# Two changes to a fused recurrence and gated MLP: four products alternate over TensorE's quadrants, and three of six inversions use 16-wide substitution

## The chip, the cores and the metric

The kernel runs on one core of one Trainium2 chip. Its time is the device time of one execution in microseconds (us); the figure for a version is the median of its runs. The engines are called as in the profile: PE is TensorE (its weight loads are PEld), DVE is VectorE, ACT is ScalarE, POOL is GpSimd and SP is the engine that issues DMAs.

## The reference

Inputs `r, k, v, w, a, b` have the shape 4 x 8 x 768 x 40 (batch, heads, tokens, head width), fp32. Each of the 32 (batch, head) pairs has a 40 x 40 state that is carried over 768 tokens. The output of that recurrence, 4 x 768 x 320, goes through a gated MLP with a product over the tokens:

```python
for t in range(S):
    y[:, :, t] = einsum('bhd,bhde->bhe', rt, state)
    Sa = einsum('bhde,bhe->bhd', state, at)
    state_decay = state * wt[:, :, None, :] - einsum('bhd,bhe->bhde', Sa, bt)
    state = state_decay + einsum('bhd,bhe->bhde', vt, kt)
x = y.transpose(0, 2, 1, 3).reshape(4, 768, 320)
h = maximum(x @ w_in, 0)                       # 320 -> 1024
u, v = h[..., :512], h[..., 512:]
v_n = (v - mean(v)) / sqrt(var(v) + 1e-6)
v_s = einsum('ts,bsd->btd', w_spatial, v_n) + b_spatial[None, :, None]
out = ((u * v_s) @ w_out)                      # 512 -> 320
```

## The kernel before

**Tiling.** The tokens of a sequence are cut into 12 chunks of 64 (`C`). Two batches run together, so that there are 24 steps (`NS`), each with one chunk of 16 (batch, head) pairs: 8 units (`NU`) on partitions 0 to 63 and 8 on 64 to 127. A half of the partitions is called `par`, and its rows `PR[par]`. In a product the two halves use either the two quadrants of TensorE on the diagonal (rows and columns of the same half) or the two others (rows of one half, output in the other).

**Inside a chunk** the recurrence becomes a triangular system. Its 64 x 64 unit lower triangle is split in two blocks of 32 (`HB`). The strict lower parts of the diagonal blocks of 4 chunks (`GS`), 32 units for each of four 32-row strips, stand in one tile `Lc` (`lprime`, L318, and `lblock`, L332). `invert(g)` (L342) inverts them for a group of 4 steps on DVE: it transposes `Lc` so that one unit's matrix lies along the free dimension of a partition, does forward substitution in place with 30 pairs of a product and a sum (L351, L355), and transposes the result twice, into `XT0` (L360) and `X11` (L362). Group 0 is inverted ahead of the steps. Groups 1 to 5 are generators whose pieces are spread over the steps before their use. `b_l21`, `b_zt`, `b_xcopy` and `b_x21` (L452 to L513) build the full 64 x 64 inverse `xf` from the two blocks; `b_x21` needs `zt`, which ACT copies out of PSUM in `b_zt_out` (L486).

**A step `s`** is a chain: `c_bp` (products with the state `Mc`, L535, diagonal quadrants), `c_ff` (L553), `c_xx` (with the inverse, L571, diagonal quadrants), `c_mp` (state update, L603) with `c_mp_out` on DVE, and `c_y` (L627) with `c_y_out` on DVE (L640), which frees the PSUM tile that the next step's `c_bp` writes. ACT copies each product out of PSUM (`c_bp_out` L545, `c_ff_out` L561, `c_xx_out` L582), and POOL's `strict` (L396) zeroes the upper triangle of some of them. For the step that follows, the same step forms `b_lka` (L389, operands `sl` and `at`; the two quadrants off the diagonal) and `b_h` (L419, operand `lin`; also off the diagonal). Each has its drain, `b_lka_out` (L406) and `b_h_out` (L429): two ACT copies and two `strict` on POOL.

**Preparation.** `scan1`, `scan2`, `at_mul` and `sl_mul` (L281 to L313) prepare chunks 4 to 23 on DVE, two per step up to step 3 and then one. `decode` turns the 64-bit `w_in` into a pair of fp32r values on DVE in steps 4 to 10. From step 11 the MLP's first product fills PE (`m_u` L742, `m_v` L697), one piece at each of the four times `M1` to `M4` of a step. What is left of it, and phase 2 (`spatial` L173 to L180 and `proj` L193), follows the last step.

**What sets the order.** In phase 1 the order of every engine's queue is written out: `at(t, fn, ...)` enters a call at time `t` in units of steps, the list is sorted, and the calls are issued in that order. [...] The times of this kernel for a step `s`: `c_bp` 0.00 and 0.05 for its two groups of 4 units, `b_lka` 0.115, `b_lka_out` 0.17 and 0.19, `c_ff` 0.30 and 0.35, `c_xx` 0.55 and 0.60, `c_xx_out` 0.60 and 0.65, `b_zt` 0.66, `b_h` 0.68, `b_zt_out` 0.68, `b_h_out` 0.72 and 0.74, `c_mp` 0.74 and 0.76, `b_x21` 0.78, `c_y` 0.86 and 0.90. In steps 3, 7, 11, 15 and 19, where the next step begins a group, `b_zt` is at 0.88 and `b_x21` at 1.12. Behind the last step the order is the scheduler's. PSUM tiles of `ps_k` (two buffers) are shared by `lprime`, `b_lka`, `b_h`, `b_tok`, `b_l21`, `b_zt` and `b_x21`.

Of the kernel before, what the change touches and what calls it, by code (L numbers as in the profile page):

```python
# [211 lines left out]
def phase1(ctx, tc, early, late, vtok, win, xs, vns, uts, dscr):  # L212
# [39 lines left out]
    maskp = const.tile([P, C], F32, name="maskp")
    maskn = const.tile([P, C], F32, name="maskn")
# [87 lines left out]

    def invert(g):  # L342
        Lc = st.pop(("Lc", g))
# [3 lines left out]
        nc.vector.memset(A.rearrange("p t s -> p (t s)")[:, 0:HB * HB:HB + 1], 1.0)
        for k in range(1, HB - 1):
            m = HB - 1 - k
            tp = ps_i.tile([P, m, k], F32, name="itmp")  # L350
            nc.vector.tensor_tensor(  # L351
                out=tp, in0=A[:, k + 1:, k:k + 1].broadcast_to([P, m, k]),
                in1=A[:, k:k + 1, 0:k].broadcast_to([P, m, k]), op=ALU.mult,
            )
            nc.vector.tensor_tensor(out=A[:, k + 1:, 0:k], in0=A[:, k + 1:, 0:k], in1=tp, op=ALU.add)  # L355
# [4 lines left out]
        nc.vector.transpose(out=XT0.rearrange("p u t -> p t u"), in_=A)  # L360
        yield
        nc.vector.transpose(out=X11.rearrange("p u t -> p t u"), in_=A.rearrange("p t s -> p s t"))  # L362
# [20 lines left out]

    def b_lka(s):
        Et, at, sl = st["pre", s]
        pk = ps_k.tile([P, NU, C], F32, name="bk")
        for n in range(NU):
            for par in range(2):
                nc.tensor.matmul(  # L389
                    pk[PR[1 - par], n, :], lhsT=sl[PR[par], n, 1 - par, :], rhs=at[PR[par], n, :],  # L390
                    start=True, stop=True,
                )
        st["pk", s] = pk

# [6 lines left out]
    def b_lka_out(s, par):  # L401
        At = st["blk", s][0]
        pk = st["pk", s]
        ev = PR[1 - par]
        if s in LKA_POOL:
            nc.scalar.activation(At[par][ev], pk[ev], AF.Copy)  # L406
            strict(At[par][ev], NU)
            return
        nc.vector.tensor_tensor(
            out=At[par][ev], in0=pk[ev],  # L410
            in1=maskp[ev].unsqueeze(1).broadcast_to([64, NU, C]), op=ALU.mult,
        )

    def b_h(s):
# [1 line left out]
        ph = ps_k.tile([P, NU, C], F32, name="bk")
        for n in range(NU):
            for par in range(2):
                nc.tensor.matmul(  # L419
                    ph[PR[1 - par], n, :], lhsT=li[RR[par], n, 0:C], rhs=li[RR[par], n, C:2 * C],  # L420
                    start=True, stop=True,
                )
        st["ph", s] = ph

    def b_h_out(s, par):
        ev = PR[1 - par]
        Rt = Rts[s % 2]
        if s in H_POOL:
            nc.scalar.activation(Rt[par][ev, :, 0:C], st["ph", s][ev], AF.Copy)  # L429
            strict(Rt[par][ev, :, 0:C], NU)  # L430
            return
        nc.vector.tensor_tensor(
            out=Rt[par][ev, :, 0:C], in0=st["ph", s][ev],
            in1=maskp[ev].unsqueeze(1).broadcast_to([64, NU, C]), op=ALU.mult,
        )

# [92 lines left out]
    def c_bp(s, g):  # L529
        gp, ns = grp(g)  # L530
        li = lin[s % 2]
        bp = ps_b.tile([P, NP, NR], F32, name=f"bp{g}")
        for q, n in enumerate(ns):
            for par in range(2):
                nc.tensor.matmul(  # L535
                    bp[PR[par], q, :], lhsT=Mc[RR[par], n, :], rhs=li[RR[par], n, C:],
                    start=(q == 0), stop=False, skip_group_check=True,
                )
# [37 lines left out]
    def c_xx_out(s, g):  # L576
        gp, ns = grp(g)
        Rt = st["blk", s][1]
        xx = st["xx", g]
        if s in TRI_POOL:  # L580
            for par in range(2):
                nc.scalar.activation(Rt[par][PR[par], gp], xx[PR[1 - par]], AF.Copy, scale=-1.0)  # L582
            for par in range(2):
                strict(Rt[par][PR[par], gp, 0:C], NP)
            return
        for par in range(2):
            nc.scalar.activation(Rt[par][PR[par], gp, C:], xx[PR[1 - par], :, C:], AF.Copy, scale=-1.0)
        for par in range(2):
            ur, ev = PR[par], PR[1 - par]
            nc.vector.tensor_tensor(  # L590
                out=Rt[par][ur, gp, 0:C], in0=xx[ev, :, 0:C],
                in1=maskn[ev].unsqueeze(1).broadcast_to([64, NP, C]), op=ALU.mult,
            )

# [264 lines left out]
    with tc.manual_schedule():  # L859
# [20 lines left out]
        for m, val in ((maskp, 1.0), (maskn, -1.0)):  # L880
            p.memset(m, val)
            for rows in PR:
                p.affine_select(
                    out=m[rows], in_=m[rows], pattern=[[1, C]], base=0,
                    channel_multiplier=-1, compare_op=ALU.is_gt, fill=0.0,
                )
        for t in (Mc, *xfs):
# [110 lines left out]
```

## Time and profile before

| | |
|---|---|
| median of 3 runs | 706.14 us (703.38 to 710.57) |
| the profiled execution | 708.83 us, of it 707.1 us span |
| mean granted PE clock | 0.897 |
| PE, DVE, ACT, POOL busy | 584.4, 444.9, 387.8, 297.9 us |
| DMA | 87.66 MB, mean 124 GB/s |

Busy time is the union of an engine's instructions. The page shows the span in 40 equal slices (17.7 us each), a digit being a tenth of busy time. In a row of busy time by stretch there follow the stretch, its length, and for PE, PEld, DVE, ACT and POOL the busy us and in brackets the number of instructions; then the granted clock, the share of the DMA engines and GB/s. In a row of the timeline stand start, duration, engine, line, operation, output and inputs and the number of instructions; in square brackets the idle time before it and what ended it. "issue" means that no semaphore ended it. In a row of a group of instructions stand the busy time and the mean ns of one, and then the idle time before them.

### The profile page before, as it was taken

How to read it: one execution, taken by the hardware profiler on the slowest of the kernel's cores; microseconds unless marked ns; L12 is line 12 of the kernel's file. 1: busy time of each engine (PE TensorE's matmuls, PEld its weight loads, DVE VectorE, ACT ScalarE, POOL GpSimd, SP SyncE). 2: the span in 40 equal slices, each digit the busy share in tenths (PEclk: the TensorE clock that was granted, in tenths of full speed). 3: DMA queues.
4: the chain of work that ended last, by engine and by line, in shares of the span. 5: the costliest groups of instructions: out<-in, count | busy, mean ns of one | idle time of the engine just before them, and what ended most of it. 6: DMA issues, size and time to landing. Idle time of an engine off the chain costs nothing. (4 is left out here: it accounts for less than half of the span.)

```text
span 707.1 us, 25562 instructions
## 1 busy us (share of the span) xinstructions
PE 584.4 (83%) x10784; PEld 533.2 (75%) x10784; DVE 444.9 (63%) x884; ACT 387.8 (55%) x856; POOL 297.9 (42%) x486
## 2 busy tenths in 40 slices
PE   1716786477776786999998999989999999999997
PEld 1605675467666785888877788778888989999997
DVE  7898679987999999877777466611127521322221
ACT  2406463355555765587866888887855543331112
POOL 5202132113445455354653434544448982553221
PEclk9656898868887888799997999998999999999999
DMA  9562758366564644666547545454336464650001
GB/s 186 97 118 47 145 114 164 63 132 123 123 129 106 147 91 111 133 147 139 115 135 220 128 135 148 121 157 119 107 106 187 143 179 135 189 178 28 29 29 57
DMA packets 105179, 87.66 MB, mean 124 GB/s; under 512 B 34344, under 2 KB 90920, under 8 KB 103144
## 3 DMA queue, kind: packets, MB, share of 16 engines
q1 hardware_dynamic: 104520, 84.31, 48.7%
q10 hardware_dynamic: 544, 1.72, 1.1%
q8 instruction: 85, 1.39, 0.9%
q14 instruction: 30, 0.25, 0.1%
HBM read 59.20 MB, written 20.50 MB: 113 GB/s over the span
## 5 line engine op out<-in xcount | busy, mean ns | idle before, releaser
L396 POOL TENSOR_SCALAR_AFFINE_SELECT Rt<-Rt 64x512 f32<-64x512 f32 (+1 forms) x144 | 85.1, 592 | 105.6 <-ACT Rt L582 73.9
L545 ACT ACTIVATE Rt<-bp 64x416 f32<-64x416 f32 x96 | 49.2, 513 | 72.6 <-PE bp L535 71.0
L396 POOL TENSOR_SCALAR_AFFINE_SELECT At<-At 64x512 f32<-64x512 f32 x48 | 42.1, 877 | 83.1 <-ACT At L406 68.3
L351 DVE TENSOR_TENSOR itmp<-A 128x30 f32<-128x30 f32 (+9 forms) x180 | 70.6, 392 | 3.3
L535 PE MATMUL bp<-lin,Mc 40*64 40x104 f32 x768 | 53.6, 305 | 22.1 <-DVE y L640 21.5
L535 PEld LDWEIGHTS bp<-lin,Mc 40*64 40x64 f32 x768 | 47.0, 169 | 25.0 <-DVE y L640 24.0
L173 PE MATMUL pg<-wsh,vh 128*128 128x384 f32 x192 | 64.7, 337 | 0.0
L174 PE MATMUL pg<-wsl,vh 128*128 128x384 f32 x192 | 64.7, 337 | 0.0
L175 PE MATMUL pg<-wsh,vl 128*128 128x384 f32 x192 | 64.6, 336 | 0.0
L355 DVE TENSOR_TENSOR A<-A,itmp 128x30 f32<-128x30 f32 (+9 forms) x180 | 59.1, 328 | 6.2
L177 DVE TENSOR_TENSOR g<-pg,bb 128x384 f32<-128x384 f32 x32 | 17.8, 556 | 64.6 <-PE pg L175 59.2
L54 POOL TENSOR_TENSOR gl<-g,gh 128x384 fp32r<-128x384 f32 x32 | 33.9, 1063 | 49.9 <-ACT gh L50 49.7
L582 ACT ACTIVATE Rt<-ch 64x416 f32<-64x416 f32 x96 | 49.2, 513 | 3.9 <-PE ch L571 1.5
L553 PE MATMUL ch<-Rt,At 128*64 128x104 f32 x768 | 48.5, 287 | 0.0
L553 PEld LDWEIGHTS ch<-Rt,At 128*64 128x64 f32 x768 | 43.0, 160 | 4.4 <-issue 1.7
L326 PE MATMUL bk<-at,sl 64*32 64x32 f32 x1536 | 22.3, 210 | 27.4 <-DVE sl L313 14.7
L571 PE MATMUL ch<-ffs,xf 64*64 64x104 f32 x768 | 43.4, 266 | 1.1 <-issue 1.1
L477 PE MATMUL bk<-XT,l 32*32 32x32 f32 x768 | 18.3, 198 | 30.8 <-DVE XT L360 27.7
L54 POOL TENSOR_TENSOR vl<-raw,vh 128x512 fp32r<-128x512 f32 x24 | 32.1, 1344 | 27.2 <-ACT vh L50 22.2
L50 ACT ACTIVATE gh<-g 128x384 fp32r<-128x384 f32 x32 | 16.6, 523 | 48.7 <-DVE g L178 48.7
L477 PEld LDWEIGHTS bk<-XT,l 32*32 32x32 f32 x768 | 15.5, 113 | 35.1 <-issue 23.5
L326 PEld LDWEIGHTS bk<-at,sl 64*32 64x32 f32 x1536 | 18.8, 121 | 30.6 <-DVE sl L313 14.8
(134 smaller groups left out, 1580.9 us busy)
## 6 DMA issues: line engine op xcount, KB each, us to landing
ein<-in_early SPq DMA_DIRECT2D x40, 387.0 KB
lin<-in_late SPq DMA_DIRECT2D x48, 160.0 KB
At<-at SPq DMA_DIRECT2D x48, 128.0 KB
uts<-ur SPq DMA_DIRECT2D x48, 128.0 KB
vns<-vr SPq DMA_DIRECT2D x24, 256.0 KB
raw<-vns SPq DMA_DIRECT2D x24, 256.0 KB
ut<-uts SPq DMA_DIRECT2D x24, 256.0 KB
Rt<-in_vtok SPq DMA_DIRECT2D x48, 80.0 KB
```

The costliest lines, as they stand in the source:

```text
L54: eng.tensor_tensor(out=lo, in0=x, in1=hi.bitcast(F32), op=ALU.subtract)
L173: nc.tensor.matmul(pg, lhsT=vh[:, dc], rhs=w_h, start=(i == 0), stop=False)
L174: nc.tensor.matmul(pg, lhsT=vh[:, dc], rhs=w_l, start=False, stop=False)
L175: nc.tensor.matmul(pg, lhsT=vl[:, dc], rhs=w_h, start=False, stop=(i == NT - 1))
L351: nc.vector.tensor_tensor(out=tp, in0=A[:, k + 1:, k:k + 1].broadcast_to([P, m, k]), in1=A[:, k:k + 1, 0:k].broadcast_to([P, m, k]), op=AL ...
L355: nc.vector.tensor_tensor(out=A[:, k + 1:, 0:k], in0=A[:, k + 1:, 0:k], in1=tp, op=ALU.add)
L396: nc.gpsimd.affine_select(out=t, in_=t, pattern=[[0, k], [1, C]], base=0, channel_multiplier=-1, compare_op=ALU.is_gt, fill=0.0,)
L535: nc.tensor.matmul(bp[PR[par], q, :], lhsT=Mc[RR[par], n, :], rhs=li[RR[par], n, C:], start=(q == 0), stop=False, skip_group_check=True,)
L545: nc.scalar.activation(Rt[par][PR[par], gp, :], st["bp", g][PR[par]], AF.Copy)
L553: nc.tensor.matmul(ff[PR[1 - par], q, :], lhsT=At[par][:, n, :], rhs=Rt[par][:, n, :], start=True, stop=True,)
L571: nc.tensor.matmul(xx[ev, q, :], lhsT=xf[ev, n, :], rhs=ffs[ev, q, :], start=True, stop=True,)
L582: nc.scalar.activation(Rt[par][PR[par], gp], xx[PR[1 - par]], AF.Copy, scale=-1.0)
```

## The change

Two things change, and the order with them.

**Inversion.** For groups 0, 1 and 2 (`INV16`) the substitution on DVE inverts the two 16 x 16 diagonal blocks of each 32 x 32 block side by side: 14 pairs on a view with one more dimension of 2. The block off the diagonal is left at zero on the way. `X11` is transposed ahead of `XT0`. Then, per step of data, `b_y` multiplies the lower left 16 x 16 block (from `Lc`, whose first 16 columns POOL has cleared) by the inverse, `wy` takes the product, and `b_xx` multiplies it by the other inverse, for `XT0` (32 matmuls) and for the two upper strips of `X11` (32, half of them with the identity). ACT copies them into `XT0` and `X11`. Groups 3, 4 and 5 are inverted as before. `Lc` gets a second buffer.

**Quadrants.** `b_h` of the next step is issued inside `c_bp`, and `b_lka` of the next step inside `c_xx`, unit by unit, so that matmuls on the diagonal quadrants and off them alternate. `b_h_out` moves to 0.12 and 0.14, `b_lka_out` to 0.66 and 0.665. Masks that no path uses any more are dropped.

```diff
     def invert(g):
-        Lc = st.pop(("Lc", g))
-        A = inv.tile([P, HB, HB], F32, name="A")
+        Lc = st["Lc", g]
+        wide = g in INV16
+        W = SB if wide else HB
+        At = inv.tile([P, HB * HB + HB], F32, name="A")
+        A = At[:, 0:HB * HB].rearrange("p (t s) -> p t s", s=HB)
         nc.vector.transpose(out=A, in_=Lc.rearrange("p u t -> p t u"))
         yield
+        nc.vector.memset(At[:, 0:HB * HB:HB + 1], 1.0)
+        if wide:
+            nc.gpsimd.memset(Lc[:, :, 0:SB], 0.0)
+            nc.vector.memset(A[:, SB:, 0:SB], 0.0)
+        nb = HB // W
+        D = At.rearrange("p (b x) -> p b x", b=2)[:, :, 0:SB * HB]
+        D = D.rearrange("p b (t s) -> p b t s", s=HB) if wide else A.unsqueeze(1)
+        for k in range(1, W - 1):
+            m = W - 1 - k
+            tp = ps_i.tile([P, nb, m, k], F32, name="itmp")
             nc.vector.tensor_tensor(
+                out=tp, in0=D[:, :, k + 1:W, k:k + 1].broadcast_to([P, nb, m, k]),
+                in1=D[:, :, k:k + 1, 0:k].broadcast_to([P, nb, m, k]), op=ALU.mult,
             )
+            nc.vector.tensor_tensor(
+                out=D[:, :, k + 1:W, 0:k], in0=D[:, :, k + 1:W, 0:k], in1=tp, op=ALU.add
+            )
             yield
...
+    def b_y(s):
...
+        m4 = ps_k.tile([P, NU, SB], F32, name="bk")
+        for n in range(NU):
+            for o in range(0, P, HB):
+                nc.tensor.matmul(
+                    m4[o:o + HB, n, :], lhsT=Lc[o:o + HB, u0 + n, :], rhs=X11[o:o + HB, u0 + n, 0:SB],
+                    start=True, stop=True,
+                )
+        nc.scalar.activation(wy[:, :, 0:SB], m4, AF.Copy)
+
+    def b_xx(s):
...
+        m5 = ps_k.tile([P, 2, NU, SB], F32, name="bk")
+        for n in range(NU):
+            for o in range(0, P, HB):
+                nc.tensor.matmul(
+                    m5[o:o + HB, 0, n, :], lhsT=wy[o:o + HB, n, :], rhs=XT0[o:o + HB, u0 + n, SB:],
+                    start=True, stop=True,
+                )
+        for n in range(NU):
+            for o in (0, 64):
+                nc.tensor.matmul(
+                    m5[o:o + HB, 1, n, :], lhsT=XT0[o:o + HB, u0 + n, :], rhs=wy[o:o + HB, n, 0:SB],
+                    start=True, stop=False, skip_group_check=True,
+                )
+            for o in (0, 64):
+                nc.tensor.matmul(
+                    m5[o:o + HB, 1, n, :], lhsT=ident[o:o + HB, o:o + HB],
+                    rhs=X11[o:o + HB, u0 + n, 0:SB], start=False, stop=True, skip_group_check=True,
+                )
+        nc.scalar.activation(XT0[:, us, SB:], m5[:, 0], AF.Copy)
+        for o in (0, 64):
+            nc.scalar.activation(X11[o:o + HB, us, 0:SB], m5[o:o + HB, 1], AF.Copy)
...
     def c_bp(s, g):
...
+            if s + 1 < NS:
+                b_h(s + 1, n)
...
     def c_xx(s, g):
...
+            if s + 1 < NS:
+                b_lka(s + 1, n)
...
-            at(b + 0.17 + 0.02 * par, b_lka_out, q, par)
-            at(b + 0.72 + 0.02 * par, b_h_out, q, par)
+            at(b + 0.66 + 0.005 * par, b_lka_out, q, par)
+            at(b + 0.12 + 0.02 * par, b_h_out, q, par)
...
-        at(b + 0.115, b_lka, q)
...
-        at(b + 0.68, b_h, q)
...
         t1 = GS * g - 1 + 0.70
         gen = invert(g)
-        for k in range(INV_N):
-            at(t0 + (t1 - t0) * k / (INV_N - 1), step, gen)
+        if g in INV16:
+            t1 -= 0.30
+        for k in range(inv_n(g)):
+            at(t0 + (t1 - t0) * k / (inv_n(g) - 1), step, gen)
+        for k in range(GS if g in INV16 else 0):
+            at(t1 + 0.08 + 0.30 * k, b_y, GS * g + k)
+            at(t1 + 0.20 + 0.30 * k, b_xx, GS * g + k)
...
+        for q in range(GS):
+            t = (0.30, 0.47, 0.90, 1.20)[q]
+            at(t, b_y, q)
+            at(t + 0.02, b_xx, q)
```

More of the change, by code (lines that the diff above doesn't have):

```diff
@@ L219, in phase1 @@
     LV = slice(0, 64 + E)
+    SB = HB // 2
+    INV16 = (0, 1, 2)
     def pool(name, bufs=1, **kw):
@@ L251, in phase1 @@
     ident = const.tile([P, P], F32, name="ident")
[L252 to L253 removed]
+    wy = const.tile([P, NU, HB], F32, name="wy")
     Mc = const.tile([P, NU, C], F32, name="Mc")
@@ L333, in lblock @@
         if s % GS == 0:
-            st["Lc", s // GS] = inv.tile([P, GS * NU, HB], F32, name="Lc")
+            st["Lc", s // GS] = inv.tile([P, GS * NU, HB], F32, name="Lc", bufs=2)
         Lc = st["Lc", s // GS]
@@ L342, in invert @@
     def invert(g):
-        Lc = st.pop(("Lc", g))
-        A = inv.tile([P, HB, HB], F32, name="A")
+        Lc = st["Lc", g]
[3 more added lines that the diff above has]
+        A = At[:, 0:HB * HB].rearrange("p (t s) -> p t s", s=HB)
         nc.vector.transpose(out=A, in_=Lc.rearrange("p u t -> p t u"))
         yield
[L347 to L350, printed above, removed]
+        nc.vector.memset(At[:, 0:HB * HB:HB + 1], 1.0)
[8 more added lines that the diff above has]
+            tp = ps_i.tile([P, nb, m, k], F32, name="itmp")
             nc.vector.tensor_tensor(
-                out=tp, in0=A[:, k + 1:, k:k + 1].broadcast_to([P, m, k]),
-                in1=A[:, k:k + 1, 0:k].broadcast_to([P, m, k]), op=ALU.mult,
-            )
-            nc.vector.tensor_tensor(out=A[:, k + 1:, 0:k], in0=A[:, k + 1:, 0:k], in1=tp, op=ALU.add)
+                out=tp, in0=D[:, :, k + 1:W, k:k + 1].broadcast_to([P, nb, m, k]),
+                in1=D[:, :, k:k + 1, 0:k].broadcast_to([P, nb, m, k]), op=ALU.mult,
+            )
+            nc.vector.tensor_tensor(
+                out=D[:, :, k + 1:W, 0:k], in0=D[:, :, k + 1:W, 0:k], in1=tp, op=ALU.add
+            )
             yield
@@ L359, in invert, with inv_n @@
         st["X", g] = (XT0, X11)
+        nc.vector.transpose(out=X11.rearrange("p u t -> p t u"), in_=A.rearrange("p t s -> p s t"))
+        yield
         nc.vector.transpose(out=XT0.rearrange("p u t -> p t u"), in_=A)
         yield
-        nc.vector.transpose(out=X11.rearrange("p u t -> p t u"), in_=A.rearrange("p t s -> p s t"))
-        yield
-    INV_N = HB + 1
+    def inv_n(g):
+        return 1 + (SB if g in INV16 else HB)
+    def b_y(s):
+        XT0, X11 = st["X", s // GS]
+        Lc = st["Lc", s // GS]
+        u0 = (s % GS) * NU
+        m4 = ps_k.tile([P, NU, SB], F32, name="bk")
[7 more added lines that the diff above has]
+    def b_xx(s):
+        XT0, X11 = st["X", s // GS]
+        u0 = (s % GS) * NU
+        us = slice(u0, u0 + NU)
+        m5 = ps_k.tile([P, 2, NU, SB], F32, name="bk")
[19 more added lines that the diff above has]
+            nc.scalar.activation(X11[o:o + HB, us, 0:SB], m5[o:o + HB, 1], AF.Copy)
     def lin_load(s):
@@ L382, in b_copy, with b_lka @@
         nc.sync.dma_start(out=st["blk", s][0][par][PR[par]], in_=at[PR[par]])
-    def b_lka(s):
+    def b_lka(s, n):
         Et, at, sl = st["pre", s]
[L386 to L393, printed above, removed]
+        if n == 0:
+            st["pk", s] = ps_k.tile([P, NU, C], F32, name="bk")
+        for par in range(2):
+            nc.tensor.matmul(
+                st["pk", s][PR[1 - par], n, :], lhsT=sl[PR[par], n, 1 - par, :], rhs=at[PR[par], n, :],
+                start=True, stop=True,
+            )
     def strict(t, k):
@@ L404, in b_lka_out, with b_h @@
         ev = PR[1 - par]
[L405 to L414, printed above, removed]
-        li = lin[s % 2]
[L416 to L423, printed above, removed]
+        nc.scalar.activation(At[par][ev], pk[ev], AF.Copy)
+        strict(At[par][ev], NU)
+    def b_h(s, n):
+        li = lin[s % 2]
+        if n == 0:
+            st["ph", s] = ps_k.tile([P, NU, C], F32, name="bk")
+        for par in range(2):
+            nc.tensor.matmul(
+                st["ph", s][PR[1 - par], n, :], lhsT=li[RR[par], n, 0:C], rhs=li[RR[par], n, C:2 * C],
+                start=True, stop=True,
+            )
     def b_h_out(s, par):
@@ L427, in b_h_out @@
         Rt = Rts[s % 2]
[L428 to L435, printed above, removed]
+        nc.scalar.activation(Rt[par][ev, :, 0:C], st["ph", s][ev], AF.Copy)
+        strict(Rt[par][ev, :, 0:C], NU)
     def b_tok(s, h):
@@ L579, in c_xx_out @@
         xx = st["xx", g]
[L580 to L585, printed above, removed]
         for par in range(2):
-            nc.scalar.activation(Rt[par][PR[par], gp, C:], xx[PR[1 - par], :, C:], AF.Copy, scale=-1.0)
+            nc.scalar.activation(Rt[par][PR[par], gp], xx[PR[1 - par]], AF.Copy, scale=-1.0)
         for par in range(2):
[L589 to L593, printed above, removed]
+            strict(Rt[par][PR[par], gp, 0:C], NP)
     def c_mp(s, g):
@@ L761, in phase1 @@
     AT_ENG, SL_ENG, LO_ENG, XC = v, v, p, act_copy
-    H_POOL, LKA_POOL, TRI_POOL = range(0, 99), range(0, 99), range(0, 99)
     M1, M2, M3, M4 = 0.22, 0.46, 0.65, 0.80
@@ L879, in phase1 @@
         make_identity(nc, ident)
[L880 to L887, printed above, removed]
+        for t in (Mc, wy, *xfs):
             p.memset(t, 0.0)
@@ L894, in phase1 @@
                 )
+        for o in range(0, P, HB):
+            nc.scalar.activation(
+                wy[o:o + HB, :, SB:],
+                ident[o:o + HB, o + SB:o + HB].unsqueeze(1).broadcast_to([HB, NU, SB]), AF.Copy,
+            )
         for q in range(GS):
@@ L907, in phase1 @@
             if q == 1:
-                b_lka(0)
+                for n in range(NU):
+                    b_lka(0, n)
                 b_tok(0, 0)
@@ L922, in phase1 @@
         prep_load(5, 48)
-        b_h(0)
+        for n in range(NU):
+            b_h(0, n)
         for _ in invert(0):
```

2 lines of the change are left out of this document (1 added, 1 removed).

## The prediction

> **What bounds the kernel now.** I read the page first, its first two parts.
>
> ```profile
> PE 584.4 (83%) x10784; PEld 533.2 (75%) x10784; DVE 444.9 (63%) x884; ACT 387.8 (55%) x856; POOL 297.9 (42%) x486
> ...
> PE   1716786477776786999998999989999999999997
> DVE  7898679987999999877777466611127521322221
> ...
> PEclk9656898868887888799997999998999999999999
> ```
>
> PE's 83% is an average over two regimes. In slices 0 to 15 (to about 280 us) DVE is the fuller engine and the granted clock sags; after that PE is nearly full at full clock. So I split the first phase at the first `c_bp` matmul of each step and asked for the busy time of these stretches. These nine are steps 1 to 8, and step 18 as one of the later kind; x is the number of instructions.
>
> ```profile
> 71.87:94.99 23.12, 17.04 (x462) 15.62 (x456) 12.22 (x18) 11.85 (x27) 4.99 (x8) 0.78 0.56 101
> 94.99:116.13 21.14, 13.42 (x465) 11.95 (x457) 20.13 (x40) 11.52 (x27) 6.60 (x8) 0.96 0.87 173
> 116.13:146.16 30.03, 17.10 (x424) 15.57 (x424) 28.69 (x61) 11.06 (x25) 4.54 (x8) 0.73 0.42 78
> 146.16:167.32 21.16, 16.57 (x488) 15.05 (x489) 13.86 (x30) 12.06 (x27) 4.57 (x8) 0.82 0.93 186
> 167.32:186.54 19.22, 14.79 (x397) 13.51 (x393) 18.58 (x36) 11.80 (x27) 9.49 (x10) 0.86 0.40 93
> 186.54:207.26 20.72, 15.44 (x393) 14.06 (x393) 20.17 (x40) 12.04 (x27) 9.87 (x10) 0.83 0.65 135
> 207.26:228.00 20.74, 15.20 (x360) 13.98 (x361) 20.29 (x36) 11.65 (x25) 9.35 (x10) 0.75 0.42 101
> 228.00:247.71 19.71, 15.81 (x424) 14.27 (x424) 19.30 (x36) 12.44 (x29) 8.61 (x10) 0.85 0.63 143
> ...
> 424.89:442.42 17.53, 16.71 (x360) 14.80 (x360) 11.52 (x29) 15.14 (x33) 8.70 (x17) 1.00 0.54 149
> ```
>
> Steps 2, 3, 5, 6, 7 and 8 are DVE's (18.6 to 28.7 us busy of 19.2 to 30.0); steps 1 and 4 are not. Step 18 has PE at 16.7 and ACT at 15.1 of 17.5, both near the bound. How PE loses its time in a DVE step stands in the timeline; beside it is a loss of another kind:
>
> ```profile
> 201.41 1.04 PE L326 MATMUL bk<-at,sl 64*32 64x32 f32 x64
> 207.26 0.96 PE L535 MATMUL bp<-lin,Mc 40*64 40x104 f32 x8 [4.81 <-DVE y L640]
> ...
> 77.80 1.54 PE L389 MATMUL bk<-at,sl 64*64 64x64 f32 x22 [4.24 <-issue]
> ...
> 167.07 0.32 PE L326 MATMUL bk<-at,sl 64*32 64x32 f32 x5 [3.73 <-issue]
> ...
> q8 instruction: 85, 1.39, 0.9%
> ...
> 90.50:110.50 20.00, 17.91 (x616) 16.17 (x616) 17.22 (x32) 12.93 (x31) 7.80 (x10) 0.91 0.71 143
> ```
>
> At 207 PE waits 4.8 us for DVE's last product. At 77.8 and 167.1 it stops in the middle of a group and waits for nothing that the profile shows. Queue 8 carried 85 packets of 16.4 KB for PE's 21,568 instructions, some 254 per packet, so I read these stops as instructions that had not arrived. The densest 20 us that I found hold 1,232 PE instructions, 62 per us. That is my supply limit: an observed highest rate, not a proven one. [...]
>
> **The change: the inversion.** One group costs DVE this:
>
> ```profile
> L351 DVE TENSOR_TENSOR itmp<-A 128x30 f32<-128x30 f32 (+9 forms) x180 | 70.6, 392 | 3.3
> ...
> L355 DVE TENSOR_TENSOR A<-A,itmp 128x30 f32<-128x30 f32 (+9 forms) x180 | 59.1, 328 | 6.2
> ...
> L360 DVE STREAM_TRANSPOSE XT<-A 128x1024 f32<-128x1024 f32 x6 | 11.7, 1948 | 0.1
> ...
> 55.57 1.93 DVE L362 STREAM_TRANSPOSE X<-A 128x1024 f32<-128x1024 f32 x1
> ...
> L351 DVE TENSOR_TENSOR itmp<-A 128x84 f32<-128x84 f32 x12 | 4.3, 360 | 0.2
> ...
> L355 DVE TENSOR_TENSOR A<-A,itmp 128x84 f32<-128x84 f32 x12 | 2.9, 242 | 0.4
> ```
>
> Now: (70.6+59.1)/6 = 21.6 for 30 pairs, (3.3+6.2)/6 = 1.6 of gaps, three transposes of 1.95. After: 14 pairs on 2·m·k elements, 28 to 112, which I price all as the 84-element pair: 14 x 0.60 = 8.4; the transposes stay, a memset adds perhaps 0.2. A wide group saves 21.6+1.6-8.4-0.2 = 14.6 us of DVE, less perhaps half a microsecond of gaps that remain: 14. POOL's memset of `Lc` waits for the first transpose; queued behind it are only `strict` calls that PE wants later, so 0, or about 0.5 if not.
>
> **What it adds to PE.** A matmul of the program is two MATMULs and two LDWEIGHTS:
>
> ```profile
> L535 PE MATMUL bp<-lin,Mc 40*64 40x104 f32 x768 | 53.6, 305 | 22.1 <-DVE y L640 21.5
> ```
>
> `c_bp` issues 16 matmuls a step, 384 in 24 steps, and the trace has 768. `b_y` has 32, `b_xx` 64: together 384 instructions, half of a plain step's 786 (step 6), in each of steps 0 to 11 of data. Their array time is short; at 62 per us their supply is 6.2 us. ACT gets four short copies each, about 1.2 us, beside its 12 of 20 us. Where two merges fall in a step, PE's supply is the term:
> - Step 0 (merges 0, 1, 2): X11, which ends at 57.5 (55.57+1.93), comes ahead of XT0 and 14.5 + 1.9 us earlier, at about 41. From there to step 1 the order holds about 1,900 PE instructions by my count of its calls, 30.6 us at 62 per us, so 71.8, as now; what is already fetched during the long wait can take up to 7 off. I take -5 (bounds -7 and +3).
> - Step 1 (merge 3): 918+384 = 1,302, 21.1 us against 23.1: -2.
> - Step 2: DVE up to here does about 19.5: -1.6.
> - Step 3 (merges 4, 5): `b_y` waits for X11 until about 12 us in; the rest of 848+768 instructions takes about 15.5 more, 27.5 against 30.0: -2.5.
> - Step 4 (6, 7): 977+768 = 1,745, 28.3 us against 21.2: +7.2.
> - Steps 5 and 6 (none): DVE falls by 4 to 5 to about 15.5, PE's own path is as long; 16 each: -8.
> - Step 7 (8, 9): 721+768 = 1,489, 24.2 us, some of it inside the wait for DVE: +2 (0 to +3.5).
> - Step 8 (10, 11): 1,616, 26.2 against 19.7, DVE's 19.3 hidden: +6.5.
> - Steps 9, 10: DVE's third inversion is unchanged: 0.
> Sum -3.4. At 55 per us the sum is about +12. If the supply isn't the limit, a merge costs some 2.5 us (192 MATMULs, at most the 16 ns each of L326's 64 in 1.04 us): step 0 wins 7, step 1 3, step 3 4.5, and steps 4, 7 and 8 lose 4, 1 and 1.5, in all about -18.
>
> **The four quadrants.**
>
> ```profile
> L389 PE MATMUL bk<-at,sl 64*64 64x64 f32 x768 | 37.4, 266 | 4.2 <-issue 4.2
> ...
> L419 PE MATMUL bk<-lin 40*64 40x64 f32 x768 | 29.6, 230 | 0.0
> ...
> 327.15 0.27 PE L389 MATMUL bk<-at,sl 64*64 64x64 f32 x2
> 327.23 0.26 PE L535 MATMUL bp<-lin,Mc 40*64 40x104 f32 x2
> 327.26 0.28 PE L389 MATMUL bk<-at,sl 64*64 64x64 f32 x3
> ```
>
> Where `c_bp` now meets `b_lka`, the rows interleave: one uses the two diagonal quadrants, the other the two others, and neither is slowed. So `b_h` inside `c_bp` and `b_lka` inside `c_xx` should vanish: (37.4+29.6)/24 = 2.8 us of PE a step at most. But the drains move on ACT's queue: `b_lka_out` goes from ahead of `c_ff_out` to between `c_xx_out` and `b_zt_out`, and `b_h_out` takes its old place. Step 18, ACT and then PE:
>
> ```profile
> 437.59 1.05 ACT L582 ACTIVATE Rt<-ch 64x416 f32<-64x416 f32 x2
> 438.66 0.76 ACT L486 ACTIVATE zt<-bk 32x256 f32<-32x256 f32 x2
> 439.33 1.19 ACT L429 ACTIVATE Rt<-bk 64x512 f32<-64x512 f32 x2
> ...
> 438.69 0.51 PE L603 MATMUL ch<-tk,Rt 128*40 128x40 f32 x16 [0.46 <-ACT Rt L582]
> 439.48 0.69 PE L504 MATMUL bk<-zt,X 32*32 32x32 f32 x32 [0.28 <-ACT zt L486]
> ```
>
> `b_x21` (L504) starts when `zt` is out, and behind it on PE are queued the model's matmuls, `c_y` and the next `c_bp`. `b_lka_out`, as large as L429's 1.19 us, now stands ahead of `zt`. Against it stands what `b_lka` no longer takes ahead of `c_ff`, at most 1.56 (37.4/24), seldom more than 0.8 since ACT is late too: +0.4 (0 to +1.2) in nine of the steps 11 to 22. In the three (11, 15, 19) whose `b_zt` comes after `c_mp`: -0.7. Sum +1.5. `b_h` now needs `lin` 0.68 of a step earlier and `b_h_out` writes `Rt` while the token load into its other columns is under way:
>
> ```profile
> 415.79 1.78 SPq L370 DMA_DIRECT2D lin<-in_late  x2
> ...
> 426.52 1.28 SPq L374 DMA_DIRECT2D Rt<-in_vtok  x2
> ```
>
> `lin` is issued 9 us ahead of step 18 (424.89): 0. The tokens are issued after it began; the columns differ, so I take 0, and 2 us a step if ACT had to wait for them. No DMA is moved on SP's queue.
>
> Together -3.4 + 1.5, about -2, on the profiled execution's 708.83 us (span 707.1). The median, 706.14, lies 2.7 lower: 704, and I say 703 since step 0 may keep more. The second phase is untouched.
>
> **Rivals.** *The clock falls in the late steps (slower).*
>
> ```profile
> 370.60:374.00 3.40, 1.40 (x48) 1.26 (x48) 2.96 (x6) 1.47 (x3) 2.02 (x5) 1.00 0.70 191
> 374.00:377.40 3.40, 1.78 (x23) 1.46 (x19) 0.51 (x1) 1.36 (x3) 0.00 (x0) 0.50 0.96 294
> ```
>
> After a stretch with PE 1.4 of 3.4 busy the clock was halved. The new waits at `c_mp` and `b_x21` are up to 2 us close together, since `b_h` no longer fills them. It decides when PE is under about 0.6 busy there; two such stretches at half speed lose 3.4 us; in five steps +17, 704+17 = 721. For it: such a window exists. Against: most late steps have fill matmuls. *The supply doesn't bind, and the late steps gain* (faster): -18, and if ACT keeps up -1 us in twelve steps: 706-30 = 676. For it: 62 per us is only the densest seen. Against: ACT ends its chain without gaps in step 18. *The quadrants don't overlap* (the change doesn't do what it says): `b_h` then delays ACT's first copies, about 1.1 us, and the 1.2 is paid in full in nine steps: 12 x 1.1 + 9 x 0.8, 704+20 = 724. The row of the seam speaks against it. [...]
>
> **Chances.** Forecast 0.44 (own range 692 to 714), supply free 0.24, clock 0.23, no overlap 0.09. One per cent, 7 us, is about what can be told from no change. The forecast gives 0.36, 0.54 and 0.10 of itself to faster, same and slower; the rivals fall almost wholly on their sides: faster 0.40, same 0.28, slower 0.32. The range that leaves out a tenth on each side is 675 to 726.
>
> **What would show it.** Inversion: DVE busy lower by about 40. Supply: PE idle put down to "issue" inside `b_y`, `b_xx` or just after, steps 4 and 8 longer than now. Quadrants: `b_h` rows between `c_bp`'s without a longer union. ACT: L504 waiting longer for `zt`. Clock: halved stretches after 290 us. I am wrong if steps 4 and 8 stay at 20 us, or if the late steps shrink by 1 us or more.

## The result, and the profile after

The changed kernel takes 760.92 us (755.77 to 763.55 in 4 runs); the kernel before, beside it, 704.76 us (702.19 to 710.57). The ratio is 1.078, with a 95% interval of 1.069 to 1.087: slower by 56 us. I had said 703, with a range of 675 to 726.

The first lines of the page after (busy time and number of instructions by engine, then tenths in 40 slices of 19.0 us):

```profile
PE 622.6 (82%) x13088; PEld 560.0 (74%) x13088; DVE 409.4 (54%) x791; ACT 396.9 (52%) x908; POOL 290.0 (38%) x484
...
PE   2657775868777966697896888887899999999997
...
DVE  8861479424987729976867745551215431142221
...
PEclk9555687656866579689888789889999999999999
```

DVE gave up 35.5 us (444.9 to 409.4), as meant. The row of the clock is the news: in slices 1 to 15 (counted from 0) it stands mostly at 5 to 8 where it stood mostly at 8, and in slices 16 to 28, where it was 9 almost throughout, there are dips to 6, 7 and 8.

By stretches from the first `c_bp` of one step to that of the next; these are steps 2, 3, 4, 5, 7, 8 and 18 (the columns are those of the table before):

```profile
102.97:121.89 18.92, 13.56 (x463) 11.34 (x457) 17.90 (x35) 11.49 (x27) 8.46 (x9) 0.86 0.89 181
121.89:157.59 35.70, 23.86 (x809) 21.58 (x809) 19.37 (x35) 12.85 (x33) 4.48 (x8) 0.64 0.63 118
157.59:189.31 31.72, 26.32 (x879) 24.02 (x873) 12.99 (x26) 13.87 (x35) 4.82 (x9) 0.57 0.28 63
189.31:206.59 17.28, 12.77 (x400) 10.93 (x392) 16.62 (x32) 11.67 (x27) 9.22 (x10) 0.87 0.54 129
...
226.56:253.10 26.54, 22.43 (x748) 20.49 (x745) 17.52 (x23) 12.74 (x32) 10.06 (x10) 0.63 0.34 85
253.10:284.91 31.81, 23.88 (x815) 21.63 (x809) 17.99 (x34) 15.08 (x39) 7.94 (x10) 0.62 0.32 75
...
475.27:495.38 20.11, 17.44 (x363) 15.19 (x361) 11.17 (x28) 14.47 (x34) 8.59 (x17) 0.84 0.46 130
```

Steps 2 and 5, which DVE set before and in which no merge falls, are shorter (18.92 from 21.14, 17.28 from 19.22). A merge is `b_y` and `b_xx` for one step of data. Steps 3, 4, 7 and 8, with two merges each, are 5.7, 10.6, 5.8 and 12.1 us longer, at a clock of 0.57 to 0.64; step 0, with three, is 8.4 us longer at 0.57. Step 18, which has no merge at all, is 2.6 us longer, at 0.84 where it had 1.00. So there are two losses. Put together from such stretches:

| | before | after | difference |
|---|---|---|---|
| up to step 0 | 29.95 | 28.70 | -1.3 |
| steps 0 to 10 | 258.45 | 298.23 | +39.8 |
| steps 11 to 22 | 231.66 | 251.08 | +19.4 |
| step 23 and phase 2 | 187.04 | 183.79 | -3.3 |

**The early loss.** A merge in step 4, and the clock over it (timeline of PE, then windows of 3.41 us: the trace's clock changes 53 times, always at multiples of 3,413 ns, and these windows lie on that grid):

```profile
157.10 0.55 PE L327 MATMUL bk<-at,sl 64*32 64x32 f32 x25 [4.53 <-issue]
...
160.55 1.05 PE L387 MATMUL bk<-X,Lc 32*32 32x16 f32 x64
...
164.09 1.05 PE L400 MATMUL bk<-XT,wy 32*32 32x16 f32 x64 [0.97 <-ACT Rt L474]
...
233.96 0.73 PE L387 MATMUL bk<-X,Lc 32*32 32x16 f32 x64
```

```profile
157.84:161.25 3.41, 3.41 (x116) 3.16 (x116) 3.31 (x5) 1.02 (x2) 0.00 (x0) 0.50 0.04 10
161.25:164.67 3.42, 2.00 (x104) 1.75 (x100) 1.80 (x3) 2.88 (x7) 1.12 (x2) 0.50 0.50 125
164.67:168.08 3.41, 3.41 (x116) 3.37 (x110) 0.00 (x0) 0.70 (x4) 0.19 (x1) 0.50 1.10 248
168.08:171.49 3.41, 2.41 (x57) 2.03 (x56) 0.00 (x0) 0.52 (x1) 0.00 (x0) 0.50 0.57 119
```

L387 is `b_y`, L400 the first part of `b_xx`. Their 64 MATMULs take 1.05 us here and 0.73 us at 233.96, at full clock. PE is busy all through the windows at 157.84 and 164.67, and still the window behind each is granted half the clock. Ahead of it, at 157.1, PE had stopped 4.53 us with no cause that the profile shows.

**The late loss.** Step 18 again, PE and then ACT:

```profile
486.71 0.51 PE L637 MATMUL ch<-tk,Rt 128*40 128x40 f32 x16
488.62 0.57 PE L637 MATMUL ch<-tk,Rt 128*40 128x40 f32 x16 [1.41 <-ACT Rt L625]
490.12 1.46 PE L544 MATMUL bk<-zt,X 32*32 32x32 f32 x32 [0.92 <-ACT zt L526]
```

```profile
487.52 1.04 ACT L625 ACTIVATE Rt<-ch 64x416 f32<-64x416 f32 x2
488.60 1.21 ACT L458 ACTIVATE At<-bk 64x512 f32<-64x512 f32 x2
489.70 0.76 ACT L526 ACTIVATE zt<-bk 32x256 f32<-32x256 f32 x2
```

```profile
485.52:488.93 3.41, 2.00 (x70) 1.71 (x68) 1.63 (x3) 3.29 (x7) 1.68 (x5) 1.00 0.40 119
488.93:492.35 3.42, 2.41 (x48) 2.06 (x42) 2.07 (x7) 1.48 (x4) 1.93 (x3) 0.50 0.42 130
492.35:495.76 3.41, 3.41 (x48) 3.03 (x51) 0.69 (x2) 1.22 (x4) 0.00 (x0) 0.50 0.12 40
```

`b_h` no longer stands between `b_zt` and `c_mp` (L637), and the second group of `c_mp` waits 1.41 us; `b_lka_out` (L458) stands ahead of `zt`, and `b_x21` (L544) waits 0.92. The window holding the first of these waits is 2.00 of 3.41 busy, 0.59, and the next two run at half clock: `b_x21` takes 1.46 us where it took 0.69. It starts 14.85 us into the step, against 14.59 before (439.48 less 424.89). So up to `b_x21` the new order cost 0.3 us here, what the alternation saved being taken off, and the 2.3 us that remain of the 2.6 come behind it, where the same matmuls run at half clock.

### The profile page after: what moved, and what is told of

Same layout as the page of the kernel before. It is cut to its first block, busy times and chain, and to the rows that moved or that the text cites. A ratio compares the mean times of both kernels' runs of the same rounds, so it can differ in the third digit from the quotient of the medians.

```text
span 761.8 us, 30148 instructions
## 1 busy us (share of the span) xinstructions
PE 622.6 (82%) x13088; PEld 560.0 (74%) x13088; DVE 409.4 (54%) x791; ACT 396.9 (52%) x908; POOL 290.0 (38%) x484
## 3 DMA queue, kind: packets, MB, share of 16 engines
q10 hardware_dynamic: 544, 1.72, 1.1%
## 5 line engine op out<-in xcount | busy, mean ns | idle before, releaser
L449 POOL TENSOR_SCALAR_AFFINE_SELECT Rt<-Rt 64x512 f32<-64x512 f32 (+1 forms) x144 | 88.7, 616 | 271.2 <-ACT Rt L625 124.8
L575 PEld LDWEIGHTS bp<-lin,Mc 40*64 40x64 f32 x768 | 46.3, 168 | 11.5 <-DVE y L674 8.3
L595 PE MATMUL ch<-Rt,At 128*64 128x104 f32 x768 | 53.3, 298 | 0.8 <-ACT Rt L587 0.3
L650 DVE TENSOR_TENSOR mn<-ch,Mc 104x160 f32<-104x160 f32 x44 | 14.1, 322 | 68.8 <-PE ch L637 55.6
L361 DVE TENSOR_TENSOR itmp<-A 128x108 f32<-128x108 f32 (+15 forms) x132 | 48.5, 367 | 2.1
L466 PE MATMUL bk<-lin 40*64 40x64 f32 x768 | 46.2, 276 | 3.9 <-DMA lin<-in_late 3.9
L674 DVE TENSOR_TENSOR y<-bp,Et 104x256 f32<-104x256 f32 x48 | 20.1, 421 | 52.0 <-PE bp L661 51.9
L613 PE MATMUL ch<-ffs,xf 64*64 64x104 f32 x768 | 46.9, 279 | 0.0
L449 POOL TENSOR_SCALAR_AFFINE_SELECT At<-At 64x512 f32<-64x512 f32 x48 | 38.6, 804 | 19.7 <-ACT At L458 17.8
L466 PEld LDWEIGHTS bk<-lin 40*64 40x64 f32 x768 | 39.9, 166 | 4.4 <-DVE A L365 2.6
L613 PEld LDWEIGHTS ch<-ffs,xf 64*64 64x64 f32 x768 | 41.1, 152 | 1.5 <-ACT Rt L625 0.2
```

The costliest lines, as they stand in the source:

```text
L361: nc.vector.tensor_tensor(out=tp, in0=D[:, :, k + 1:W, k:k + 1].broadcast_to([P, nb, m, k]), in1=D[:, :, k:k + 1, 0:k].broadcast_to([P, nb ...
L449: nc.gpsimd.affine_select(out=t, in_=t, pattern=[[0, k], [1, C]], base=0, channel_multiplier=-1, compare_op=ALU.is_gt, fill=0.0,)
L466: nc.tensor.matmul(st["ph", s][PR[1 - par], n, :], lhsT=li[RR[par], n, 0:C], rhs=li[RR[par], n, C:2 * C], start=True, stop=True,)
L575: nc.tensor.matmul(bp[PR[par], q, :], lhsT=Mc[RR[par], n, :], rhs=li[RR[par], n, C:], start=(q == 0), stop=False, skip_group_check=True,)
L595: nc.tensor.matmul(ff[PR[1 - par], q, :], lhsT=At[par][:, n, :], rhs=Rt[par][:, n, :], start=True, stop=True,)
L613: nc.tensor.matmul(xx[ev, q, :], lhsT=xf[ev, n, :], rhs=ffs[ev, q, :], start=True, stop=True,)
```

## The experiments

My theory after the result: the merges run at half clock and don't raise it, and in the late steps two waits that `b_h` used to cover let the clock fall. The rivals: the supply of PE's instructions, as I had predicted; the order of ACT's queue alone; the waits between DVE, `b_y`, ACT and `b_xx`. "The run before" below is always the kernel before on the same chip, at 707 to 708 us. Two small edits are in every run but the kernel before and the run with the order of the fill alone: `mn` in `c_mp_out` has one buffer in place of two, and `X11` is transposed first in every group. They don't make the late loss: in the profiles of the five runs below with the late steps otherwise as before, steps 11 to 22 take 230 to 239 us, against 231.7 before. This spread is also what a difference between two profiles of late steps has to exceed.

### Each part alone

```diff
 # the inversion alone: blocks at their old places
-            if s + 1 < NS:
-                b_h(s + 1, n)
...
-            if s + 1 < NS:
-                b_lka(s + 1, n)
...
-            at(b + 0.66 + 0.005 * par, b_lka_out, q, par)
-            at(b + 0.12 + 0.02 * par, b_h_out, q, par)
+            at(b + 0.17 + 0.02 * par, b_lka_out, q, par)
+            at(b + 0.72 + 0.02 * par, b_h_out, q, par)
...
+        for n in range(NU):
+            at(b + 0.115, b_lka, q, n)
+            at(b + 0.68, b_h, q, n)
```

> Only the 16-wide inversions and the merges; b_lka and b_h are issued as blocks at their old places. If the merges make the loss of steps 0 to 10 (39.8 us in the profiles), because they run at half clock and do not raise it: 705 + 35 to 45, so 740 to 750, steps 11 to 22 within 0.5 us each of before. If the alternation of the quadrants is what costs in the early steps too: under 715.

```diff
 # the quadrants alone
-    INV16 = (0, 1, 2)
+    INV16 = ()
...
-        for q in range(GS):
+        for q in range(GS if 0 in INV16 else 0):
             t = (0.30, 0.47, 0.90, 1.20)[q]
```

> Only the alternation; all six groups are inverted as before. If the two parts add up: the late steps lose the 19.4 us of the profiles and the early steps stay, 705 + 15 to 25, so 720 to 730. If the late loss comes with the merges (their instructions or their clock carried on): within 7 us of 705. If the early steps gain where b_h is hidden: 710 to 718.

The inversion alone: 742.68 us, ratio 1.051 (1.045 to 1.058), 34.9 over the run before. The quadrants alone: 729.23 us, 1.030 (1.025 to 1.036), 21.4 over it. Together 56.3, and the whole change lost 56.2: within the intervals, some 4 to 6 us for each run, the parts add up. In the profiles the inversion lost 33.9 us in steps 0 to 10 and 5.6 in steps 11 to 22, which is inside the spread, and the quadrants 3.2 and 19.8.

### The late steps: two orders

```diff
 # zt first
-            at(b + 0.66 + 0.005 * par, b_lka_out, q, par)
+            at(b + 0.70 + 0.005 * par, b_lka_out, q, par)
```

> The run with the quadrants alone, with b_lka_out entered behind b_zt_out (0.70 in place of 0.66). If the late loss is the order of ACT's queue (b_x21 waits for zt behind b_lka_out): 12 to 20 us under the run with the quadrants alone. If it is the clock that falls after the wait of c_mp and the wait of b_x21 together: the wait of 1.4 us at c_mp stays, and only the steps whose window comes out above some 0.6 busy recover: 3 to 10 us under it.

```diff
 # the fill in the wait
-    M1, M2, M3, M4 = 0.22, 0.46, 0.65, 0.80
+    M1, M2, M3, M4 = 0.22, 0.46, 0.65, 0.75
```

> The run with the quadrants alone, with the fourth piece of the MLP in a step entered at 0.75, between the two groups of c_mp, in place of 0.80, behind b_x21. No work is added or taken away. If the clock falls because PE waits there: the window stays above 0.6 busy, PE keeps its full clock over 290 to 540 us, and 12 to 22 us are won against the run with the quadrants alone. If ACT's order sets the late steps and the clock is only a companion: within 3 us of it.

709.78 us (ratio to before 1.002, 0.998 to 1.005) and 706.30 us (0.999, 0.996 to 1.003): each of the two edits takes the whole loss of the quadrants away, 19 and 23 us, though one reorders ACT and the other PE. The waits of PE over steps 11 to 22 for `c_mp` (L637) and `b_x21` (L544), in us, times and the longest, for the quadrants alone, with `zt` first, and with the fill:

```profile
PE ch L637 <- ACT Rt L625: 12.8, 14, 2.0
PE bk L544 <- ACT zt L526: 10.7, 14, 1.6
```

```profile
PE ch L637 <- ACT Rt L625: 13.9, 16, 1.9
...
PE bk L544 <- ACT zt L526: 3.2, 8, 0.8
```

```profile
PE bk L544 <- ACT zt L526: 3.5, 8, 0.9
...
PE ch L637 <- ACT Rt L625: 3.0, 6, 1.2
```

With `zt` first the wait at `c_mp` is as large as it was and that of `b_x21` 7.5 us smaller (a third one, of `b_l21` for ACT, fell from 9.0 to 4.3 us). Steps 11 to 22 as a whole, in the same order of runs:

```profile
291.70:543.20 251.50, 215.21 (x4622) 183.63 (x4618) 136.36 (x300) 180.44 (x404) 114.24 (x225) 0.88 0.48 128
```

```profile
289.10:521.60 232.50, 205.66 (x4624) 175.98 (x4616) 135.79 (x299) 179.42 (x403) 109.10 (x222) 0.92 0.52 139
```

```profile
287.40:520.70 233.30, 206.41 (x4640) 177.63 (x4628) 135.50 (x302) 182.07 (x404) 111.22 (x226) 0.93 0.52 139
```

Neither edit takes work away, and 19.0 and 18.2 us went. About half of that, 9.5 and 8.8 us, is busy time of PE: the same matmuls ran faster. The other half is waiting that is gone, so the waits cost by themselves too, beside the clock. Within these steps a full clock was halved 11 times with the quadrants alone, 7 times with `zt` first, 6 times with the fill, and twice before. The wait at `c_mp` can do it by itself: in step 17 of the run with `zt` first it is 1.72 us long, `b_x21` waits for nothing, and the clock falls behind a window that was 1.70 of 3.42 us busy:

```profile
423.40 0.63 PE L637 MATMUL ch<-tk,Rt 128*40 128x40 f32 x16 [1.72 <-ACT Rt L625]
```

```profile
420.19:423.61 3.42, 1.70 (x60) 1.18 (x61) 1.72 (x3) 2.96 (x6) 1.33 (x4) 1.00 0.51 154
423.61:427.02 3.41, 3.26 (x56) 2.98 (x50) 2.58 (x6) 1.58 (x4) 1.97 (x4) 0.50 0.70 229
```

So it was enough to shorten the second wait, or to fill both. No run takes away the wait at `c_mp` and leaves that of `b_x21`. My expectation that `zt` alone would recover only 3 to 10 us was wrong: I had counted only the clock, and not the waits of `b_x21` and `b_l21` themselves, which are half of the gain.

> The quadrants alone with both orders mended: b_lka_out behind b_zt_out (0.70) and the fourth MLP piece between the groups of c_mp (0.75). If the alternation is worth something once no wait is left in the late steps: 690 to 702. If each of the two orders removes the same loss: like the runs with one of them, 702 to 711.

Both edits together: 699.09 us, 0.989 (0.985 to 0.993). This is the fastest version found that leaves nothing out, 9 us under before. But part of that does not belong to the alternation:

```diff
 # the kernel before, with this alone
-    M1, M2, M3, M4 = 0.22, 0.46, 0.65, 0.80
+    M1, M2, M3, M4 = 0.22, 0.46, 0.65, 0.75
```

> The kernel before with nothing but the fourth piece at 0.75 in place of 0.80. If the 9 us won by the alternation with both orders mended come from the alternation: within 4 us of before. If they come from the place of the piece: 695 to 702.

702.01 us, 0.992 (0.988 to 0.996): one number in the kernel before gives some 5 of the 9 us. Its profile does not show them in the waits: steps 11 to 22 take 233.42 us, 1.8 more than before, with 16 MATMULs of phase 2 that came later before; what follows is 4.1 us shorter, and steps 0 to 10, which the edit does not touch, are 3.0 shorter. Where the 5 us come from stays open. Between 0.989 and 0.992 the intervals overlap, so what the alternation adds to it, some 3 us, is not settled. That it does shorten PE is plain: with both orders mended PE was busy 200.81 us in steps 11 to 22, before 216.88, that is 1.3 us a step at the least, of the 2.8 that I gave as the most.

```diff
 # b_h alternates, b_lka as a block
             if s + 1 < NS:
                 b_h(s + 1, n)
...
-            if s + 1 < NS:
-                b_lka(s + 1, n)
...
-            at(b + 0.66 + 0.005 * par, b_lka_out, q, par)
+            at(b + 0.17 + 0.02 * par, b_lka_out, q, par)
...
+        for n in range(NU):
+            at(b + 0.115, b_lka, q, n)
```

> Only b_h alternates with c_bp; b_lka and b_lka_out are at their old places, the fourth piece at 0.75, all groups inverted as before. ACT then has neither b_h_out nor b_lka_out behind c_xx_out, and b_x21 waits for nothing else than b_zt_out. If that end of ACT's queue and the cover at c_mp are what the late steps need: 691 to 699, at or below the run with both orders mended (699). If hiding b_lka is worth its 1.5 us in each late step too: 700 to 708.

714.28 us, 1.012 (1.006 to 1.018), longer than both expectations. Steps 12, 16 and 20 are 3.6, 0.6 and 5.4 us longer than with both orders mended. In them a new wait stands: `b_x21` of the first step of a group, issued at 1.12, waits for the drain of `b_h` (L474). The two share the PSUM buffers of `ps_k`, which I take to be the reason.

```profile
PE bk L544 <- ACT Rt L474: 5.9, 3, 2.6
```

It accounts for 6 of the 15 us by which this run is longer; what made the rest stays open.

> The whole change with the two orders of the late steps mended (0.70 for b_lka_out, 0.75 for the fourth piece). If the two parts do not touch each other: 699 + 35 = 734, within 6 us. If the merges gain from the alternation in the early steps (b_h and b_lka hidden beside c_bp and c_xx leave PE room): under 725.

The whole change with both orders: 735.03 us, 1.042 (1.034 to 1.050), within 1 us of the 734 expected. So the inversion loses 35 to 36 us in both surroundings.

### The early steps: what a merge costs

```diff
 # no merges: the blocks off the diagonal are not formed
-        for k in range(GS if g in INV16 else 0):
+        for k in range(0):
             at(t1 + 0.08 + 0.30 * k, b_y, GS * g + k)
...
-        for q in range(GS):
+        for q in range(0):
             t = (0.30, 0.47, 0.90, 1.20)[q]
```

> The inversion alone, with b_y and b_xx left out, PE's and ACT's part: the blocks off the diagonal of the inverse are not formed. What is left of the change is what DVE saves. If DVE's 14 us a group are worth what the prediction took (step 0 the whole 14, and 2 to 4 us in each of steps 2, 3, 5, 6, 7, 8, 9 and 10): 708 less 25 to 40, so 668 to 683, and the merges cost 60 to 75. If DVE's time is mostly hidden: 695 to 706, and the merges cost 37 to 48.

675.01 us, 0.956 (0.949 to 0.963). DVE's saving is worth 32 us, in the middle of the expected 25 to 40. The twelve merges then cost 742.68 - 675.01 = 67.7 us, 5.6 us each. Steps 0 to 10 without the merges and with them:

```profile
29.70:254.00 224.30, 169.20 (x4647) 152.93 (x4643) 191.08 (x348) 133.48 (x305) 88.15 (x107) 0.83 0.66 134
```

```profile
30.20:322.60 292.40, 222.04 (x6948) 201.77 (x6946) 189.33 (x348) 145.78 (x353) 84.37 (x107) 0.75 0.50 103
```

And the two largest groups of stops of PE by "issue" (us, times, longest), without the merges and then with them:

```profile
PE bk L327 <- issue: 8.6, 4, 4.1
PE bk L443 <- issue: 4.5, 1, 4.5
```

```profile
PE bk L327 <- issue: 19.1, 8, 4.6
...
PE bk L406 <- issue: 8.2, 4, 4.4
```

Of the 68.1 us between the two stretches 52.8 are PE's busy time and 15.3 its idle time. All stops put down to "issue" together are 16.1 us without merges and 32.3 with them, so the supply makes up as much as the idle part; what the chain of DVE, `b_y`, ACT and `b_xx` added in waits, other waits gave back. As for the busy part, a merge at full clock takes about 0.73 + 0.73 + 1.1 = 2.6 us by the rows of this kernel's own merges, 31 us for twelve. Some 22 us of busy time are left, which is an estimate of what half clock costs, for the merges and for the matmuls beside them. The next pair measures the clock by itself.

```diff
 # wide matmuls ahead of each b_y: rows is 128 or 32
     def b_y(s):
...
+        for _ in range(3):
+            nc.tensor.matmul(
+                m4[:, NU:, :].rearrange("p n s -> p (n s)").rearrange("p (a c) -> p a c", a=3),
+                lhsT=ident[0:rows, :], rhs=ident[0:rows].unsqueeze(1).broadcast_to([rows, 3, P]),
+                start=True, stop=True, skip_group_check=True,
+            )
```

> The inversion alone, with three matmuls of 384 columns and 128 active rows added ahead of each of the 12 b_y; what they compute is overwritten or never read. They add 24 us of PE at full clock. If the merges run slowly because small matmuls, though back to back, don't bring the clock up: PE's lost clock in steps 0 to 10 falls from 73 us to under 60, and the time is 742 + 0 to 12. If the clock doesn't depend on what the matmuls do: 742 + 20 to 45.

> As the run with 128 rows, but the same added matmuls have 32 active rows; count, columns and order are the same. If the clock follows the rows and columns at work: the windows stay at half clock, the lost clock in steps 0 to 10 is over 80 us, and the run is 10 to 30 us slower than the one with 128 rows. If it follows busy time alone: the two are within 5 us of each other.

With 128 rows 753.39 us (ratio to before 1.069, 1.061 to 1.078), with 32 rows 775.07 (1.100, 1.092 to 1.108): 21.7 us apart, for the same instructions in the same places. The groups of the added matmuls (L386) and of the first part of `b_xx` (L407 here), first with 128 rows, then with 32; busy time and mean of one:

```profile
L386 PE MATMUL bk<-ident 128*128 128x384 f32 x72 | 38.2, 686 | 2.1 <-issue 1.1 <-ACT tk L494 0.9
...
L407 PE MATMUL bk<-XT,wy 32*32 32x16 f32 x768 | 9.4, 184 | 8.7 <-issue 3.6 <-DVE XT L374 1.9 <-ACT xf L560 1.8
```

```profile
L386 PE MATMUL bk<-ident 32*128 32x384 f32 x72 | 40.4, 714 | 0.5 <-ACT tk L494 0.5
...
L407 PE MATMUL bk<-XT,wy 32*32 32x16 f32 x768 | 12.4, 207 | 6.7 <-issue 2.8 <-ACT xf L560 1.8 <-ACT wy L398 1.2
```

```profile
156.95:160.36 3.41, 3.41 (x94) 2.17 (x88) 1.12 (x3) 1.28 (x4) 1.42 (x3) 1.00 0.03 6
160.36:163.78 3.42, 3.42 (x136) 3.19 (x134) 0.85 (x2) 0.75 (x2) 0.00 (x0) 0.50 0.50 118
```

The added matmuls themselves are busy for nearly the same time, 38 and 40 us. With 128 rows the run is only 10.7 us longer than the inversion alone: 27 us of the 38 came back. In steps 0 to 10 PE's other work took 20 us less busy time (240.24 - 38.2 = 202.0, against 222.04 in the row above; the first part of `b_xx` 9.4 us in place of 11.5) at a mean clock of 0.82 in place of 0.75, which is near the estimate of 22; the rest was idle time that the added matmuls filled. With 32 rows 8 us came back, and the other work ran no faster (265.08 - 40.4 = 224.7, at a clock of 0.72). The last fence, of the run with 32 rows, shows a window at full clock in which PE was busy without a break (3.41 of 3.41 us), and the clock is halved behind it all the same. So the clock does not follow busy time alone: with the same instructions, the number of active rows changed it, 0.82 with 128 rows against 0.72 with 32 over steps 0 to 10.

```diff
 # a third of the instructions: the products are others than the reference's
-            for o in range(0, P, HB):
-                nc.tensor.matmul(
-                    m4[o:o + HB, n, :], lhsT=Lc[o:o + HB, u0 + n, :], rhs=X11[o:o + HB, u0 + n, 0:SB],
+            nc.tensor.matmul(
+                m4[:, n, :], lhsT=Lc[L32, u0 + n // 4 * 4:u0 + n // 4 * 4 + 4, :].rearrange("p n t -> p (n t)"),
+                rhs=X11[L32, u0 + n, 0:SB], start=True, stop=True,
...
```

> The inversion alone, with b_y and b_xx in 128 instructions in place of 384: one matmul with 32 active rows and 128 columns stands for the four of a unit's quadrants, so that the products are others than the reference's. If the number of instructions (their supply and their time on PE) is the loss of 34 us in steps 0 to 10: 698 to 715, and no stop put down to issue in those steps beyond those of before. If the loss lies in the waits of the chain DVE, b_y, ACT, b_xx, ACT: 725 to 742.

836.47 us, 1.188 (1.179 to 1.197), far outside both expectations. The reason is the replacement, not the theory: a matmul that loads 128 columns of weights for 16 columns of data is 2.7 to 3.4 times as dear as the four that it replaces.

```profile
62.00 3.59 PE L387 MATMUL bk<-X,Lc 32*128 32x16 f32 x16 [0.45 <-ACT tk L485]
...
84.79 1.95 PE L387 MATMUL bk<-X,Lc 32*128 32x16 f32 x16
```

One takes 224 ns at half clock and 122 at full, where four on 32 x 32 quadrants take 4 x 1.05/64 = 66 and 4 x 0.73/64 = 46. Of the supply the run tells a little: with a third of the merges' instructions no stop by "issue" is left inside the merges, and all such stops in steps 0 to 10 fall from 32.3 to 13.1 us. For the waits of the chain it decides nothing.

## Why the prediction was wrong

| step | forecast | the change | the inversion alone |
|---|---|---|---|
| 0 | -5 | +8.4 | +6.5 |
| 1 | -2 | +0.9 | +0.5 |
| 2 | -1.6 | -2.2 | -2.3 |
| 3 | -2.5 | +5.7 | +5.8 |
| 4 | +7.2 | +10.6 | +12.1 |
| 5 and 6 | -8 | -2.7 | -4.7 |
| 7 | +2 | +5.8 | +5.2 |
| 8 | +6.5 | +12.1 | +12.4 |
| 9 and 10 | 0 | +1.3 | -1.6 |
| 11 to 22 | +1.5 | +19.4 | +5.6 |

**DVE's saving: right.** 14 us a group were forecast, about 40 us of busy time in all; DVE lost 35.5, X11 let `b_y` start at 41.06 us (forecast about 41), and the saving alone is worth 32 us.

**The price of a merge: wrong, and this is the step that failed.** The sum of -3.4 for steps 0 to 10 with a saving of about 34 (258.5 to 224.3 without merges) means that I charged some 31 us for twelve merges, 2.6 each. They cost 68. I had taken the densest 20 us of the kernel before, 62 instructions per us at a clock of 0.91, for the rate at which any dense stretch would run, and gave the clock no term of its own in these steps. The steps with two merges ran at 45 (step 3), 55 (4), 56 (7) and 51 (8), counting both columns of x in the rows above; even the 55 per us that I tried as a lower rate gave only +12. The largest single miss is step 0, with three merges: -5 forecast, +8.4 measured. What I named as the limit is there: the stops put down to "issue" are 16 us longer with the merges than without. The nine that are over 1 us long in steps 0 to 10 of the trace after, 1.2 to 5.2 us, each end 1.4 to 1.6 us after a packet of queue 8 has landed; the one at 157.10 ends 1.41 us after a packet that landed at 155.69. But the larger part, by the estimate above, is PE at half clock, though clocks of 0.73 to 0.86 stood in seven of the rows that I quoted for steps 1 to 8. My 2.5 us for a merge without a limit of supply is what it takes at full clock; nine or ten of the twelve ran at half.

**The quadrants overlap: right.** Rows 495.77 and 495.82 of the trace after show `c_bp` and `b_h` side by side, a pair of each every 89 ns as in the seam:

```profile
495.77 0.25 PE L575 MATMUL bp<-lin,Mc 40*64 40x104 f32 x2
495.82 0.23 PE L466 MATMUL bk<-lin 40*64 40x64 f32 x2
495.86 0.25 PE L575 MATMUL bp<-lin,Mc 40*64 40x104 f32 x2
```

**ACT's order: right in place, and in size where it was looked at** (0.4 forecast, 0.3 up to `b_x21` in step 18), and wrong in that I let it end there.

**The clock in the late steps: the rival that came true.** I gave it 0.23 and 17 us for the late steps; they lost 19.4. The place was the one named (`c_mp` and `b_x21` close together, with `b_h` gone), and the point from which it decides, about 0.6 busy, was near: in the trace before, over steps 0 to 22, half clock followed 15 of the 16 windows at full clock that were up to 0.61 busy and none of the 87 above; in the trace after, over steps 0 to 22, half clock followed 24 of the 25 windows at full clock that were under 0.7 busy, and 1 of the other 60. That the size fits is in part luck. I had reckoned with five steps that lose 3.4 us each; the clock fell 12 times in steps 11 to 22 (twice before), ten of the twelve steps lost something, and the time that the alternation saved stands against it. What I held against this rival, that most late steps have matmuls of the model as fill, did not hold: they stand ahead of `c_mp` and behind `b_x21`, not between.

**The range.** The 721 for this rival hold -3.4 for the early steps and 17 for the late ones; with the 40 that the early steps lost it would have been 764, against 761 measured. The upper end of 726 was too low since no case carried the clock into the merges.

## What to carry to other kernels

Work moved to TensorE has to be priced at the clock that it will itself bring about, and with the stops for instructions that it brings: here small matmuls on 32 rows kept PE busy and the clock mostly at half (0.57 to 0.64 in the steps with two merges), and the merges cost 68 us where their own time at full clock is some 31. When work that filled a wait is hidden elsewhere, look for the windows of the clock that it had kept busy; here moving one independent piece of work into the gap won back the 21 us that the alternation had lost. Of the two waits it was enough to shorten the second, though the first could still halve the clock.
